# Three edits at the first tile of a retention and maxout kernel: where the tables are issued, when the scores are made, how the last products are ordered

## The chip, the cores and the metric

The kernel runs on one core of a Trainium2 chip. The metric is the device time of one execution in microseconds (us). A core has a matrix engine (TensorE, PE in the profile; its weight loads are PEld), a vector engine (VectorE, DVE), a scalar engine (ScalarE, ACT), a general engine (GpSimd, POOL) and a queue engine (SyncE, SP). Each works through its own instructions in order[...]. Products land in PSUM, eight banks of 128 x 512 fp32.

## The reference

```python
scores = scale * (q @ k.T)                      # 8 batches, 8 heads, 576 positions, 64 wide
ret = scores * gamma[h] ** (i - j), for i >= j  # 0 otherwise
attn = ret @ v
x = attn.transpose(0, 2, 1, 3).reshape(4608, 512)
h = maximum(maximum(x @ w1, x @ w2), x @ w3)    # w1, w2, w3: 512 x 768
out = h @ w_out                                 # w_out: 768 x 512
```

The four weight matrices come in as float64 (read as pairs of 32-bit words) and are made into float32 on the chip. All products are in fp32.

## The kernel before, in words

The 4608 positions are cut into 36 chunks of 128 (`C`), and four chunks make a tile of 512 (`NT`): nine tiles. The attention is done in its recurrent form, chunk by chunk:

- `load(g)` (L160) issues the transfers of k, q and v of a chunk from SP's queue. From chunk 7 on (`BY_PE`), q and k also come in blocks of 32 (`load_blocks`, L147).
- `decay_values(g)` (L164, POOL) scales v by the table `gk`, and gives `vd`.
- `transposes(g)` makes k and q transposed: below chunk 7 on PE (`kt`, `qt`, L181) with copies by ACT (L183); later by DVE (L175).
- `scores(g)` forms `s` on PE in two banks (L191), and DVE multiplies them with the causal mask into `st` (L194).
- `values(chunks, new_states)` adds `st` by `vd` (L244), forms `kv` for the next state (L211), adds the part of the old state (L256), and DVE scales the result by the table `gq` into `xT` (L263), the transposed x of the tile. `keep` (L219, L221, POOL L222) makes the next state with the table `gs`.

`convert(n)` takes n steps of a generator which turns the float64 pieces of the weights (128 x 512 each) into float32: 18 pieces of w1 to w3 and six of w_out, each four steps, with DVE (L431, L436, L442, L447, L453) and ACT (L432, L434, L437). Each finished piece frees a buffer for the next piece's load (`load_weights`, L311 and L305, SP).

Tile 0 takes the weights as they come: `up_plain` (L553) makes one 128 x 512 block of one of the three products, and DVE takes the maximum (L556; for w1 a copy by ACT, L557). A pair of blocks is a unit, and there are nine units. Then `down` makes the four row blocks of the output, each one bank with six products over all of the hidden units (L544), a copy by ACT and a store. From tile 1 on each unit is done by Strassen's scheme with seven half-sized products (`up`, L495, tiles x, y and z), and `downs` likewise (L367). These need sums of weight blocks (`weight_sums(n)` for a unit, L474 and L475 on DVE, L476 and L477 on POOL), sums of x (L273 to L276), sums of w_out (`sums_of_outs`) and of the hidden units (`sums_of_hidden`). `chores` is a list of such small works, and `up` takes one of them at three places (`chore()`).

The order of instructions is written by hand. A prelude at the end of the kernel's function (L601 to L631) does the first four chunks. The main loop (L670) then does, for each of twelve steps of a tile, the attention work that `steps(t + 1)` puts there for the next tile, and one stretch of the tile's own work (`ffn(t)` up to its next `yield`).

PSUM is divided into `ps_r` (four banks), `ps_x` and `ps_y` (two each).

Of the kernel before, what the change touches and what calls it, by code (L numbers as in the profile page):

```python
# [34 lines left out]
FP32 = mybir.dt.float32  # L35
# [7 lines left out]
C = 128  # L43
NT = 4 * C
# [7 lines left out]
def kernel(  # L52
# [14 lines left out]
    nc = tc.nc  # L67
    P = 128
    B, H, S, D = q.shape
    N, DM = out.shape  # L70
    DF = moe_w1.shape[1]
    NP = H // 2
    NG = B * S // C
    NDC = DM // P
    NF = DF // P
    CPT = NT // C
# [11 lines left out]
    opool = ctx.enter_context(tc.tile_pool(name="opool", bufs=2))  # L88
    while_converting = ExitStack()
    wraw = while_converting.enter_context(tc.tile_pool(name="wraw", bufs=WAHEAD))  # L90
    wtmp = while_converting.enter_context(tc.tile_pool(name="wtmp", bufs=4))
    ps_r = ctx.enter_context(tc.tile_pool(name="ps_r", bufs=4, space=PSUM))
    ps_x = ctx.enter_context(tc.tile_pool(name="ps_x", bufs=2, space=PSUM))
    ps_y = ctx.enter_context(tc.tile_pool(name="ps_y", bufs=2, space=PSUM))
# [3 lines left out]
    gq = const.tile([P, NP, C], FP32, name="gq")  # L98
    gs = const.tile([P, NP, D], FP32, name="gs")
# [21 lines left out]
    for r in sorted({start_of(g) for g in range(NG)} - {0, None}):  # L121
        m = masks[r] = const.tile([C, C], FP32, name=f"causal{r}")
# [15 lines left out]
    def load_blocks(g, *blocks):  # L138
        for n, src in (("q", q), ("kx", k)):

            if 0 in blocks:
                raws[n, g] = raw.tile([P, NP, C // 32, 32], FP32, tag=n, name=n + "raw", bufs=3 if n == "q" else 2)
            t = raws[n, g]
            for blk in blocks:
                b, pos = divmod(g * C + 32 * blk, S)
                for a in range(4):
                    nc.sync.dma_start(  # L147
                        t[32 * a:32 * a + 32, :, blk, :],
                        src[b, a // 2::2, pos:pos + 32, 32 * (a % 2):32 * (a % 2) + 32].rearrange("p j i -> j p i"))

    def load(g, *between):
        if g >= BY_PE and ("q", g) not in raws:
            load_blocks(g, *range(C // 32))
        for n, src in (("k", k), ("q", q), ("v", v)) if g < BY_PE else (("k", k), ("v", v)):
            if n == "v":
                for t, what in between:
                    nc.sync.dma_start(t, what)
            t = raws[n, g] = raw.tile([C, H, D], FP32, tag=n, name=n + "raw", bufs=4 if n == "k" else 3)
            for row, b, pos, m in spans(g):
                nc.sync.dma_start(t[row:row + m], src[b, :, pos:pos + m, :].rearrange("h p d -> p h d"))  # L160

    def decay_values(g):
        t = vds[g] = vpool.tile([C, H, D], FP32, tag="vd", name="vd")
        nc.gpsimd.tensor_tensor(t[:], raws.pop(("v", g))[:], gk[:].unsqueeze(2).to_broadcast([C, H, D]),  # L164
                                op=ALU.mult)
# [4 lines left out]
    def transposes(g):  # L170
        both = qks[g] = {}
        if g >= BY_PE:
            for n in ("k", "q"):
                t = both[n] = att.tile([P, NP, C], FP32, tag=n + "T", name=n + "T", bufs=2 if n == "k" else 3)
                nc.vector.transpose(t[:].rearrange("a p c -> a (p c)"),  # L175
                                    raws.pop(("kx" if n == "k" else n, g))[:].rearrange("a p b i -> a (p b i)"))
            return
        for n, src in (("k", raws["k", g]), ("q", raws.pop(("q", g)))):
            pt = ps_r.tile([P, NP, C], FP32, tag="r", name=n + "t")
            for p in range(NP):  # L180
                nc.tensor.transpose(pt[:, p, :], pair(src, p), ident[:C, :C])  # L181
            t = both[n] = att.tile([P, NP, C], FP32, tag=n + "T", name=n + "T", bufs=2 if n == "k" else 3)
            nc.scalar.copy(t[:], pt[:])  # L183

    def scores(g):
        qT, kT = qks[g]["q"], qks[g]["k"]
        s = [ps_r.tile([C, NP, C], FP32, tag="r", name=f"s{j}") for j in range(2)]
        for p in range(NP):
            for j in range(2):
                r = slice(D * j, D * (j + 1))  # L190
                nc.tensor.matmul(s[j][:, p, :], lhsT=kT[r, p, :], rhs=qT[r, p, :], start=True, stop=True)  # L191
        st = sts[g] = att.tile([C, 2, NP, C], FP32, tag="st", name="st", bufs=2)
        for j in range(2):
            nc.vector.tensor_tensor(st[:, j], s[j][:], masks[start_of(g)][:].unsqueeze(1).to_broadcast([C, NP, C]),  # L194
                                    op=ALU.mult)
# [4 lines left out]
    def half(j):  # L200
        return slice(D * j, D * (j + 1))
# [91 lines left out]
    units = [(fp, i) for fp in range(NF // 2) for i in range(3)]  # L293
    pieces = [(i, 2 * fp + e) for fp, i in units for e in range(2)] + [("out", fb) for fb in range(NF)]
    w_sb, wT, bits, to_load = {}, {}, {}, deque(pieces)
# [17 lines left out]
    late, chores = {}, deque()  # L313
# [152 lines left out]
    def weight_sums(n):  # L466
        if n >= len(units):
            return
        fp, i = units[n]
        half = [slice(0, DM // 2), slice(DM // 2, DM)]  # L470
        b11, b21 = (w_sb[i, 2 * fp][:, r] for r in half)
        b12, b22 = (w_sb[i, 2 * fp + 1][:, r] for r in half)
        t1, t2, t4 = (late["pool"].tile([P, DM // 2], FP32, name=f"T{m}_{i}_{fp}")[:] for m in (1, 2, 4))
        nc.vector.tensor_tensor(t1, b12, b11, op=ALU.subtract)  # L474
        nc.vector.tensor_tensor(t2, b22, t1, op=ALU.subtract)  # L475
        nc.gpsimd.tensor_tensor(b12, b22, b12, op=ALU.subtract)  # L476
        nc.gpsimd.tensor_tensor(t4, b21, t2, op=ALU.subtract)  # L477
        wT[fp, i] = {1: b11, 2: b21, 3: b22, 4: t4, 5: t1, 6: t2, 7: b12}
# [3 lines left out]
    def convert(n):  # L482
        for _ in range(n):
            next(converting, None)
# [53 lines left out]
            nc.vector.tensor_tensor(h[:, f0, :], h[:, f0, :], tmp[:, 0:2, :].rearrange("p a b -> p (a b)"), op=ALU.max)  # L538
        yield

    def down(t, h, m):
        ps = ps_y.tile([P, DM], FP32, tag="y", name="down")
        for fb in range(NF):
            nc.tensor.matmul(ps[:], lhsT=h[:, fb, m * P:(m + 1) * P], rhs=w_sb["out", fb],  # L544
                             start=(fb == 0), stop=(fb == NF - 1))
        osb = opool.tile([P, DM], FP32, tag="osb", name="osb")
        nc.scalar.copy(osb[:], ps[:])
        nc.sync.dma_start(out[t * NT + m * P:t * NT + (m + 1) * P, :], osb[:])

    def up_plain(t, h, fb, i):  # L550
        ps = (ps_x, ps_y)[fb % 2].tile([P, NT], FP32, tag="xy"[fb % 2], name="up")
# [7 lines left out]
    def ffn(t):  # L559

        h = hpool.tile([P, NF, NT], FP32, tag="h", name="h")
        for n, (fp, i) in enumerate(units):
            if t == 0:
                for fb in (2 * fp, 2 * fp + 1):
                    maximum = up_plain(t, h, fb, i)
                    convert(4 if i > 0 else 8 if fb % 2 == 0 else 6 if fp == 0 else 4)
                    maximum()
            else:
                if t == 1 and n == 0:
                    sums_of_outs()  # L570
                for _ in up(t, h, fp, i):
                    pass
                if i == 2:
                    sums_of_hidden(h, fp)
            yield
        if t == 0:
            convert(4 * len(pieces))
            while_converting.close()
            late["pool"] = ctx.enter_context(tc.tile_pool(name="late", bufs=1))
            for m in range(NT // P):  # L580
                down(t, h, m)
                for n in [[0, 1, 2], [3, 4, 5], [6], [7, 8]][m]:
                    weight_sums(n)
                if m < NT // P - 2:
                    yield
        else:
            chore(len(chores))
            for n, _ in enumerate(downs(t, h)):
                if n in (1, 3):
                    yield  # L590
        yield


    def tables():
        for j in range(2):
            yield gs[half(j)], state_decay[half(j), :, half(j)]
        for c in range(2):
            for b in range(2):
                yield gq[half(c), b::2, :], out_decay[half(b ^ c), NP // 2 * c:NP // 2 * (c + 1), :]

    warm(6)  # L601
    load(0)
    load(1)
    load(2, *tables())
    load(3)
    load_weights(2)
    load(4)
    load_weights(4)
    decay_values(0)
    transposes(0)  # L610
    warm(2)
    decay_values(1)
    scores(0)
    transposes(1)
    values([0], [0])
    decay_values(2)
    scores(1)
    transposes(2)
    values([1], [1])
    decay_values(3)  # L620
    scores(2)
    transposes(3)
    convert(2)
    values([2], [2])
    convert(2)
    scores(3)
    decay_values(4)
    convert(2)
    values([3], [3])
    transposes(4)  # L630
    convert(4)  # L631

    def steps(t):
# [93 lines left out]
```

## Time and profile before

| | |
|---|---|
| time, median of 3 runs | 804.61 us (803.94 to 806.73) |
| span of the profiled run | 802.5 us |
| PE, DVE, ACT, POOL busy | 98%, 52%, 22%, 18% |
| mean granted clock of PE | 0.995 |
| DMA over the span | 73 GB/s, from 0 to 40 us some 200 |
| first up product of tile 0 | at 34.73 us |
| first down product of tile 0 | at 107.51 us |
| first product of tile 1 | at 134.30 us |

The profile is one execution. Busy time is the time in which an engine had an instruction under way. Matmuls overlap, so that a busy PE need not be at its peak; whether it is, is seen from the number of products in a stretch and the time of one. An idle time is put down to what ended it ("<-" and the instruction that released it).

### The profile page before, as it was taken

What the parts mean: (1) busy time and instruction counts of PE and PEld (TensorE: products, weight loads), DVE (VectorE), ACT (ScalarE), POOL (GpSimd) and SP (SyncE); (2) the same over time, 40 slices, a digit from 0 to 9 for tenths busy, and PEclk for the clock granted to TensorE, in tenths of its full rate; (3) what the DMA queues carried; (4) which work ended last, traced back from release to release, by engine and by line L of the source; (5) the groups of instructions that cost most, each with busy time, mean ns of one, the idle gap of its engine ahead of it and who ended that gap; (6) DMA issues with size and microseconds to landing.
All of it is one profiled execution on the core that took longest, in us unless ns stands there. A gap on an engine that the chain in (4) does not pass through costs nothing.

```text
span 802.5 us, 13705 instructions
## 1 busy us (share of the span) xinstructions
PE 789.0 (98%) x5128; PEld 646.7 (81%) x5128; DVE 418.8 (52%) x833; ACT 173.7 (22%) x401; POOL 141.8 (18%) x158
## 2 busy tenths in 40 slices
PE   7899989999999999999999999999999999999998
PEld 6555436888888888888888888888888888888887
DVE  1799998545353635353544444553546344633341
ACT  2476631111111101111111111111111021111211
POOL 2200229201301121111211121112101201110000
PEclk9999999999999999999999999999999999999999
DMA  8986633333233322343233333333323323001001
GB/s 189 227 206 162 183 81 97 56 57 57 75 66 56 59 60 63 58 78 67 57 54 57 58 91 57 57 56 89 58 53 58 74 57 71 1 14 40 1 1 52
DMA packets 237506, 59.27 MB, mean 74 GB/s; under 512 B 218240, under 2 KB 236160, under 8 KB 237440
## 3 DMA queue, kind: packets, MB, share of 16 engines
q1 hardware_dynamic: 237296, 58.40, 33.3%
q8 instruction: 40, 0.66, 0.4%
q14 instruction: 26, 0.21, 0.1%
q10 hardware_dynamic: 144, 0.00, 0.0%
HBM read 48.89 MB, written 9.44 MB: 73 GB/s over the span
## 4 chain that ended last, share of the span: by engine, by line
PE 86%; DVE 5%; DMA 4%; SPq 3%; issue 1%; ACT 0%; DVEq 0%
PE x L495 32%; PE z L495 16%; PE dx L367 11%; PE y L495 8%; PE dz L367 5%; PE o L244 4%; PE s L191 3%; PE dy L367 3%; PE down L544 2%; SPq L160 2%; PE o L256 2%; PE kv L211 2%; DMA bits<-in_moe_w_dram 1%; DVE expo L447 1%; SPq L311 1%
## 5 line engine op out<-in xcount | busy, mean ns | idle before, releaser
L495 PE MATMUL x<-S,T 128*128 128x256 f32 x576 | 147.9, 379 | 0.0
L495 PEld LDWEIGHTS x<-S,T 128*128 128x128 f32 x576 | 109.1, 190 | 15.3 <-ACT p L500 0.2
L345 POOL TENSOR_TENSOR H<-h 128x256 f32<-128x256 f32 x24 | 21.3, 886 | 331.8 <-DVE h L538 331.8
L495 PE MATMUL x<-xT,w 128*128 128x256 f32 x288 | 76.1, 387 | 0.0
L495 PE MATMUL x<-S,w 128*128 128x256 f32 x288 | 74.3, 380 | 0.0
L525 DVE TENSOR_TENSOR tmp<-x,p 128x256 f32<-128x256 f32 x48 | 20.4, 425 | 103.1 <-PE x L495 103.1
L495 PE MATMUL z<-xT,T 128*128 128x256 f32 x288 | 74.0, 379 | 0.0
L495 PE MATMUL y<-xT,w 128*128 128x256 f32 x288 | 73.9, 379 | 0.0
L495 PE MATMUL z<-S,w 128*128 128x256 f32 x288 | 73.9, 379 | 0.0
L263 DVE TENSOR_TENSOR xT<-o,gq 128x512 f32<-128x512 f32 (+1 forms) x40 | 23.7, 633 | 86.5 <-PE o L256 81.1
L500 ACT COPY p<-x 128x256 f32<-128x256 f32 x72 | 26.8, 373 | 192.0 <-PE x L495 192.0
L553 PE MATMUL up<-xT,w 128*128 128x512 f32 x144 | 63.4, 595 | 0.0
L495 PEld LDWEIGHTS z<-xT,T 128*128 128x128 f32 x288 | 54.4, 189 | 8.0 <-ACT p L500 0.3
L495 PEld LDWEIGHTS y<-xT,w 128*128 128x128 f32 x288 | 54.7, 190 | 7.4
L495 PEld LDWEIGHTS z<-S,w 128*128 128x128 f32 x288 | 54.7, 190 | 7.4
L495 PEld LDWEIGHTS x<-xT,w 128*128 128x128 f32 x288 | 53.0, 190 | 9.6 <-issue 1.5
L495 PEld LDWEIGHTS x<-S,w 128*128 128x128 f32 x288 | 49.4, 189 | 13.2 <-issue 1.5
L222 POOL TENSOR_TENSOR state<-state,gs 128x256 f32<-128x256 f32 x24 | 22.0, 916 | 183.4 <-DVE state L221 179.5
L553 PEld LDWEIGHTS up<-xT,w 128*128 128x128 f32 x144 | 26.8, 190 | 31.6 <-issue 29.3
L194 DVE TENSOR_TENSOR st<-s,causal 128x512 f32<-128x512 f32 x72 | 45.0, 684 | 8.0 <-PE s L191 7.1
L500 ACT COPY u<-x 128x256 f32<-128x256 f32 x72 | 26.8, 373 | 99.8 <-PE x L495 88.8
L164 POOL TENSOR_TENSOR vd<-vraw,gk 128x512 f32<-128x512 f32 x36 | 38.3, 1064 | 45.8 <-DMA vraw<-in_v_dram 45.8
(92 smaller groups left out, 1099.4 us busy)
## 6 DMA issues: line engine op xcount, KB each, us to landing
out_dram<-osb SPq DMA_DIRECT2D x35, 256.0 KB, 2.1
kraw<-in_k_dram SPq DMA_DIRECT2D x32, 256.0 KB, 3.0
vraw<-in_v_dram SPq DMA_DIRECT2D x32, 256.0 KB, 3.5
qraw<-in_q_dram SPq DMA_DIRECT2D x464, 16.0 KB, 1.9
kxraw<-in_k_dram SPq DMA_DIRECT2D x464, 16.0 KB, 1.8
bits<-in_moe_w_dram SPq DMA_DIRECT2D x18, 256.0 KB, 4.4
bits<-in_moe_w_dram SPq DMA_DIRECT2D x36, 128.0 KB, 4.2
bits<-in_moe_w_out_dram SPq DMA_DIRECT2D x6, 512.0 KB, 4.8
```

Source lines behind the costliest of these rows:

```text
L164: nc.gpsimd.tensor_tensor(t[:], raws.pop(("v", g))[:], gk[:].unsqueeze(2).to_broadcast([C, H, D]), op=ALU.mult)
L191: nc.tensor.matmul(s[j][:, p, :], lhsT=kT[r, p, :], rhs=qT[r, p, :], start=True, stop=True)
L194: nc.vector.tensor_tensor(st[:, j], s[j][:], masks[start_of(g)][:].unsqueeze(1).to_broadcast([C, NP, C]), op=ALU.mult)
L222: nc.gpsimd.tensor_tensor(t[:], t[:], gs[:], op=ALU.mult)
L244: nc.tensor.matmul(o[n % 2][half(c), m, n // 2, :], lhsT=vds[g][:, h, :], rhs=sts[g][:, h % 2, h // 2, :], start=m == 0 and n < 2, stop=be ...
L263: nc.vector.tensor_tensor(xT[t][:, b::2, i * C:(i + len(chunks)) * C].rearrange("p u (m c) -> p u m c", c=C), o[b][:].rearrange("p m u c - ...
L345: chores.append(lambda: (pool(s3, a11, a21, op=ALU.subtract), pool(s4, a12, s2, op=ALU.subtract)))
L367: nc.tensor.matmul(out[m], lhsT=hS[n](fp)[:, m * P:(m + 1) * P], rhs=late["T"][n][:, fp, :], start=first and fp == 0 and (m == 0 or last a ...
L495: nc.tensor.matmul(out[:], lhsT=w[:, d * P:(d + 1) * P], rhs=xS[t][n][:, d, :], start=first and d == 0, stop=d == 1, skip_group_check=True)
L500: nc.scalar.copy(c[:], src[:])
L525: nc.vector.tensor_tensor(c22, x[:], p7[:], op=ALU.add)
L553: nc.tensor.matmul(ps[:], lhsT=w_sb[i, fb][:, dc * P:(dc + 1) * P], rhs=xT[t][:, dc, :], start=(dc == 0), stop=(dc == NDC - 1))
```

## The change: what it does

It has three parts.

1. *Tables by ScalarE's queue.* The tables `gs` and `gq` (six transfers of 64 KB) were issued by SP between q and v of chunk 2. They are now issued by ACT, before its first copy. SP loads chunks 0 to 4 and the weights with nothing in between.
2. *The first chunks' scores a chunk ahead.* In the prelude, the scores of a chunk come before the values of the chunk before it, so that DVE can mask them while PE is at the other. For this the transposes of chunks 0 to 4 take the banks of `ps_x`, and the scores have `ps_r` for themselves. transposes(4) now stands before values(3), and the first conversion steps come after the scores of chunk 3.
3. *Last products of tile 0 by blocks of units in four banks.* `downs_plain` has all four row blocks open at once, and goes over the six hidden blocks outermost. A w_out piece is needed only when its block is come to. Conversion steps are spread evenly (four for each up product), and the last two pieces of w_out are converted during the first two blocks. The sums of weights of units 0 to 2 are made in the last three blocks, those of units 3 to 8 in tile 1 (the second tile) as chores.

```diff
-    def load(g, *between):
+    def load(g):
...
-            if n == "v":
-                for t, what in between:
-                    nc.sync.dma_start(t, what)
...
-            pt = ps_r.tile([P, NP, C], FP32, tag="r", name=n + "t")
+            pool, tag = (ps_r, "r") if g > CPT else (ps_x, "x")
+            pt = pool.tile([P, NP, C], FP32, tag=tag, name=n + "t")
...
-    def down(t, h, m):
-        ps = ps_y.tile([P, DM], FP32, tag="y", name="down")
+    def downs_plain(t, h):
+        ps = [(ps_x, ps_y)[m % 2].tile([P, DM], FP32, tag="xy"[m % 2], name="down") for m in range(NT // P)]
         for fb in range(NF):
-            nc.tensor.matmul(ps[:], lhsT=h[:, fb, m * P:(m + 1) * P], rhs=w_sb["out", fb],
-                             start=(fb == 0), stop=(fb == NF - 1))
-        osb = opool.tile([P, DM], FP32, tag="osb", name="osb")
-        nc.scalar.copy(osb[:], ps[:])
-        nc.sync.dma_start(out[t * NT + m * P:t * NT + (m + 1) * P, :], osb[:])
+            for m, b in enumerate(ps):
+                nc.tensor.matmul(b[:], lhsT=h[:, fb, m * P:(m + 1) * P], rhs=w_sb["out", fb],
+                                 start=(fb == 0), stop=(fb == NF - 1))
+                if fb == NF - 1:
+                    osb = opool.tile([P, DM], FP32, tag="osb", name="osb")
+                    nc.scalar.copy(osb[:], b[:])
+                    nc.sync.dma_start(out[t * NT + m * P:t * NT + (m + 1) * P, :], osb[:])
+            yield
...
-                    convert(4 if i > 0 else 8 if fb % 2 == 0 else 6 if fp == 0 else 4)
+                    convert(4)
...
-            convert(4 * len(pieces))
-            while_converting.close()
-            late["pool"] = ctx.enter_context(tc.tile_pool(name="late", bufs=1))
-            for m in range(NT // P):
-                down(t, h, m)
-                for n in [[0, 1, 2], [3, 4, 5], [6], [7, 8]][m]:
-                    weight_sums(n)
-                if m < NT // P - 2:
-                    yield
+            convert(6)
+            for fb, _ in enumerate(downs_plain(t, h)):
+                convert(4 if fb < 2 else 4 * len(pieces))
+                if fb in (1, 3):
+                    yield
+                if fb == 3:
+                    while_converting.close()
+                    late["pool"] = ctx.enter_context(tc.tile_pool(name="late", bufs=1))
+                if fb > 2:
+                    weight_sums(fb - 3)
+            for n in range(3, len(units), 2):
+                chores.extend([partial(weight_sums, n), partial(weight_sums, n + 1), lambda: None])
...
-    def tables():
-        for j in range(2):
-            yield gs[half(j)], state_decay[half(j), :, half(j)]
-        for c in range(2):
-            for b in range(2):
-                yield gq[half(c), b::2, :], out_decay[half(b ^ c), NP // 2 * c:NP // 2 * (c + 1), :]
-
+    for j in range(2):
+        nc.scalar.dma_start(gs[half(j)], state_decay[half(j), :, half(j)])
+    for c in range(2):
+        for b in range(2):
+            nc.scalar.dma_start(gq[half(c), b::2, :], out_decay[half(b ^ c), NP // 2 * c:NP // 2 * (c + 1), :])
     warm(6)
-    load(0)
-    load(1)
-    load(2, *tables())
-    load(3)
+    for g in range(CPT):
+        load(g)
     load_weights(2)
-    load(4)
+    load(CPT)
     load_weights(4)
     decay_values(0)
     transposes(0)
     warm(2)
     decay_values(1)
     scores(0)
     transposes(1)
+    scores(1)
+    decay_values(2)
     values([0], [0])
-    decay_values(2)
-    scores(1)
     transposes(2)
+    scores(2)
     values([1], [1])
     decay_values(3)
-    scores(2)
     transposes(3)
+    scores(3)
     convert(2)
     values([2], [2])
     convert(2)
-    scores(3)
+    transposes(4)
     decay_values(4)
     convert(2)
     values([3], [3])
-    transposes(4)
     convert(4)
```

## The prediction

> **What bounds the kernel now.** I read the page's busy rows first, then a table of windows by stage, then TensorE's timeline from 10 to 36 us and from 106 to 136 us, then the list of waits of TensorE.
>
> ```profile
> 0.00:34.73 34.73, 26.31 (x297) 22.75 (x297) 14.36 (x30) 10.15 (x16) 8.89 (x17) 0.90 0.84 200
> 34.73:107.50 72.77, 72.77 (x338) 36.46 (x337) 71.49 (x129) 47.50 (x73) 7.89 (x6) 1.00 0.71 180
> 107.50:134.30 26.80, 24.74 (x130) 12.03 (x128) 26.39 (x37) 5.21 (x8) 19.65 (x21) 1.00 0.41 94
> 134.30:802.50 668.20, 665.21 (x4369) 575.46 (x4367) 306.55 (x640) 110.87 (x305) 105.38 (x115) 1.00 0.27 55
> ```
>
> The columns are busy us of PE, PEld, DVE, ACT and POOL, then granted clock, DMA share and GB/s. From 34.73 us (first up product of tile 0) to 107.50 PE is never idle. The 144 records at L553 are 72 products, two records each; at 0.4325 us a record (16 take 6.92 to 6.97) they are 62.3 us, and the attention pieces between them 10.2 us: 72.5 of 72.77. So PE is at its work there and not only shown busy; but DVE has 71.49 busy, nearly as full. After 134.30 PE runs to the end but for the last 3 us. What can be gained lies before 34.73 and between 107.5 and 134.3.
>
> ```profile
> 12.51 0.60 PE L181 MATMUL qt<-ident,qraw 128*128 128x128 f32 x4
> 16.75 2.26 PE L244 MATMUL o<-st,vd 128*64 128x128 f32 x15 [3.65 <-DVE st L194]
> ...
> 20.65 1.16 PE L191 MATMUL s<-qT,kT 64*128 64x128 f32 x16
> ...
> 22.77 1.40 PE L244 MATMUL o<-st,vd 128*64 128x128 f32 x15
> ...
> 25.27 1.16 PE L191 MATMUL s<-qT,kT 64*128 64x128 f32 x16
> 29.66 2.08 PE L244 MATMUL o<-st,vd 128*64 128x128 f32 x15 [3.23 <-DVE st L194]
> ...
> 33.80 0.66 PE L181 MATMUL kt<-ident,kraw 128*128 128x128 f32 x4
> ```
>
> Two stalls, 3.65 and 3.23 us, both on the masked scores `st`. The same group (o, kv, o) takes 25.27 - 22.77 = 2.50 us undisturbed, but 3.90 after the first stall and 4.14 after the second: another 1.40 and 1.64. In one-us windows the granted clock is 0.50 from 17 to 20 us and from 31 to 33.
>
> ```profile
> DVE xT L263 <- DMA gq<-in_out_decay_dram: 5.4, 2, 5.3
> PE down L544 <- DVE h L556: 1.4, 1, 1.4
> PE down L544 <- DVE w_out L453: 0.7, 1, 0.7
> ```
>
> The first stall is DVE's queue: xT of chunk 0 waits for the table gq until 14.67 and 15.25, and chunk 1's `st` stands behind it (15.93). The second: DVE converts the first weight piece from 23.05 to 28.8 ahead of chunk 3's `st`. The last two lines are the stall at the first down block, which needs all six converted w_out pieces at once.
>
> **What the Trainium skill says.** "DMA: Bandwidth & Descriptors", Issuing engines are not separate DMA queues: a second issuing engine saves only the sequencer's issue time; transfers share the same 16 engines. The trace agrees that issue time matters here: tables hold SP's queue from 8.41 to 13.4 us, and DMA share falls to 0.30 to 0.56 between 11 and 15 us. "TensorE: Matmul & The Clock Gate", Part 1: after an idle window of about 3.4 us the clock is halved. The trace agrees (0.50 after 3.65 and 3.23, still 1.00 after 1.40). "SBUF — State Buffer", Who interferes with whom: DVE with two SBUF inputs and a reading GpSimd operation block each other. The trace agrees: L474 takes 0.42 us alone, 0.94 beside POOL.
>
> **The change part by part.** Times below are the profile's; totals are estimates from them.
>
> 1. *Start of the ups.* Gone, if tables and scores come in time: 3.65 + 3.23 + 1.40 + 1.64 = 9.9 us. Four things come back.
>  (a) ACT now issues six table transfers before its table load and its first copy. One issue of such a size took 0.60 to 0.97 us at SP, once 1.35. ACT issued gk at 0.81 in 0.42; six at 0.65 end at 5.2, the load of 1.28 at 6.5, and kT of chunk 0 is copied at 6.5 in place of 5.26. Bounds: 1.2 us (0.6 each) to 5.4 (1.35 each, ACT free at 10.7). Behind the issues stand the copies kT, qT; PE's s waits for these. I take 1.2: small transfers took 0.60 at the median.
>  (b) 384 KB of tables now run beside chunk 0 and 1. At the 235 to 268 GB/s seen there these are 1.5 us, but v of chunk 2 (landed about 16.9) comes at about 13.7, since the hole of 11 to 15 us closes; chunk 3 at about 17, weight piece 0 at about 19, piece 1 at about 21. PE needs chunk 2's at about 13 to 21, so nothing is added.
>  (c) The transposes of the first five chunks go to the two ps_x banks, which kv also uses. qt of chunks 2, 3 and 4 waits for DVE to read the kv before: xT twice (0.7) and state (0.4) after the last o, less kt (0.55) on PE: about 0.5 each, 1.5 in all; bounds 0.5 and 2.5.
>  (d) transposes(4) stood after values(3), so kt and qt (0.93) hid xT of chunk 3 (0.76). Now it stands before, and the first up waits bare: 0.9.
>  DVE converts pieces 0 and 1 in the gaps, with xT of chunks 2 and 3 behind them; they land some 3 us before DVE comes to them, so no wait is added. Sum: 9.9 - 1.2 - 1.5 - 0.9 = 6.3 us; the ups start at 28.4.
>
> 2. *Ups.* PE's 72.8 us stay. The extra conversions that ran ahead (8 and 6 steps) become 4 for each product. Steps are a quarter of a piece, a piece costs DVE 2.6 us (0.34 + 0.34 + 0.6 + 0.7 + 0.6). Piece n is then written before the maximum of product n-2, that is one product (3.5 us) before PE needs it. DVE's load from start to the last maximum: 19 pieces 49.4, 12 maxima 7.2, st 4.8, states, xT and transposes 3.4, blocking by GpSimd about 4.5 (as before): 69.3 of 72.8. PE stays the bound; DVE's lead is shorter, not gone. Transfers: q and k blocks of chunk 7 must be in by about 82; SP issued the last at 88 before (needed at 97.8), and comes about 12 us earlier, as loads wait for fewer conversions. Hidden.
>
> 3. *Last products of tile 0.* 24 products at 0.865 = 20.8 us plus values 3.39 make 24.2; 26.8 were used: 2.6 us lost. With the unit of w_out outermost, the last two pieces are needed 16 products = 13.8 us into the stage, and DVE has them about 8 us in: the stall goes, -2.6. What comes: all four banks end together. ACT's third copy waits for the store of the first (two osb buffers; 2.1 us to landing), the fourth for the second, and behind them stands the copy p1 of tile 1, for which x of product 6 waits. The first block ends 2.6 us before the last, copy 0.6, issue and landing 2.5: p1 is read about 0.5 us late. +0.5 (0 to 1.5).
>
> 4. *Weight sums.* Units 0 to 2 run after values, 6 to 8 as chores in tile two. DVE takes 2 x 0.42 (0.95 contested), POOL 1.75 a unit; two such units in one up unit of 6.05 us give DVE at most 3.8 and POOL 3.5. DVE was 73% busy at 130 to 150, its other work there about 3.5 of 6 a unit, so it just fits. Product 6 of unit 0 needs t2, 8.6 us after values end; DVE has it after xT, S1, S2 at about 4.8; w of product 7 comes from POOL at 6.8, needed at 9.5. I charge 0.4 for late sums behind c22 (0 to 3).
>
> Sum: -6.3 - 2.6 + 0.5 + 0.4 = -8.0: 804.6 - 8.0 = 796.6 us.
>
> **The rivals.** *R1: DVE becomes the bound.* For: 71.49 of 72.77 busy. If its blocking costs twice the 4.5 us, its 73.8 exceeds PE's 72.8, and the short lead leaves waits at single products; with 3 more for a late chunk 7 some 4 us of the gain are lost: 800.6. Against: before, its lead grew from 0.8 us at piece 1 to 12 us at piece 17, while 3.5 extra pieces (9 us) were done.
> *R2: ACT's queue is the new wait.* Issues of 1.35 us move every copy by 5.4 in place of 1.2: 800.8. For: SP's issues of whole chunks rose to 1.62 in that stretch. Against: small ones stayed mostly at 0.60.
> *R3: slower.* Tile two starved: each of the units 0 to 2 late by 4 us through sums on DVE and POOL that must come in order, 12 us in all: 808.6. For: POOL is 100% busy from 116 to 135. Against: To chores of the same kind ran in tile two (1.5 pairs in a unit) with no PE wait.
>
> **How the numbers follow.** The forecast (795 to 798.5) 0.62; R1 0.17; R2 0.12; R3 0.04; better than forecast (put-backs at their low ends: up to 3 us less) 0.05. The range 793.6 to 801.5: below, the low ends of (c), 3 and 4 and a hidden (d); above, R1 and R2 with a little more. Faster by over 0.3% (below 802.2): 0.92, which leaves 0.04 for the upper tails of R1 and R2, within 0.3%; slower: 0.04, R3.
>
> **What would show it.** Right: no PE wait over 1.5 us before the first up, clock at 1.00 between 10 and 35 us, first up at 28 to 29.5; 72 to 73.5 us from there to the first down; no wait on w_out; 24 to 25 us from the first down to tile 1's first x. Wrong: kT of chunk 0 copied after 8 us (R2); PE waiting for L451's w within the ups (R1); waits of x, y or z for T or p1 in the first three units of tile 1 (R3).

## The result, and the profile after

The changed kernel takes 800.66 us (median of six runs, 799.61 to 800.93); the kernel before, on the same chip, 803.67 (six runs; the 804.61 given above is the median of the first three of them). The ratio is 0.9954, with a 95% interval of 0.9938 to 0.9971: about 3 us or 0.5% faster, where 8 us were forecast. A second measurement of the same kernel (below) gave 0.9959 (0.9945 to 0.9972).

The same table of windows as before, with its borders at the first up product, the first down product and the first product of tile 1. The columns are busy us of PE, PEld, DVE, ACT and POOL, granted clock, DMA share and GB/s.

```profile
0.00:30.59 30.59, 22.75 (x297) 19.06 (x297) 13.41 (x29) 10.46 (x17) 8.61 (x17) 1.00 0.91 217
30.59:103.44 72.85, 72.85 (x336) 36.52 (x337) 67.14 (x122) 43.64 (x66) 6.40 (x6) 1.00 0.73 177
103.44:127.64 24.20, 24.20 (x130) 12.20 (x129) 18.43 (x29) 8.74 (x13) 6.15 (x6) 1.00 0.46 104
127.64:797.90 670.26, 665.86 (x4369) 575.13 (x4367) 315.43 (x656) 111.36 (x306) 118.35 (x130) 1.00 0.27 56
```

Beside the table of before, border by border (us):

| stage | before | after | difference | forecast |
|---|---|---|---|---|
| to the first up product | 34.73 | 30.59 | -4.14 | -6.3 |
| ups of tile 0 | 72.77 | 72.85 | +0.08 | 0 |
| last products of tile 0 | 26.80 | 24.20 | -2.60 | -2.6 |
| tile 1 to the end | 668.20 | 670.26 | +2.06 | +0.9 |
| span | 802.5 | 797.9 | -4.6 | -8.0 |

The two profiled executions differ by 4.6 us and the medians by 3.0, because the profile of before is of a run of 804.17 us (0.5 above its median) and that of after is of the fastest of its six (1.05 below its median).

PE's timeline of the changed kernel before the first up shows what came in place of the two stalls on `st` (start, us, what, and in brackets the idle time before and what ended it):

```profile
7.73 1.16 PE L189 MATMUL s<-qT,kT 64*128 64x128 f32 x16 [0.64 <-ACT qT L181]
...
11.26 1.16 PE L189 MATMUL s<-qT,kT 64*128 64x128 f32 x16 [0.67 <-ACT qT L181]
...
14.78 0.66 PE L179 MATMUL qt<-ident,qraw 128*128 128x128 f32 x4 [0.29 <-DVE state L217]
16.12 1.16 PE L189 MATMUL s<-qT,kT 64*128 64x128 f32 x16 [0.68 <-ACT qT L181]
...
20.59 0.63 PE L179 MATMUL qt<-ident,qraw 128*128 128x128 f32 x4 [0.64 <-PE kt L179]
21.89 1.16 PE L189 MATMUL s<-qT,kT 64*128 64x128 f32 x16 [0.67 <-ACT qT L181]
...
26.36 0.63 PE L179 MATMUL qt<-ident,qraw 128*128 128x128 f32 x4 [0.64 <-PE kt L179]
...
30.59 7.10 PE L555 MATMUL up<-xT,w 128*128 128x512 f32 x16 [1.52 <-ACT expo L432]
```

No single wait is long, and the clock stays at 1.00. But there are four waits of the scores for the copy qT that was just made (the first of them, of chunk 0, comes from ACT's table issues), three of qt for a bank of `ps_x`, and one before the first up. Two of the three waits of qt are put down to PE's own kt; DVE reads the bank as `state`, which ends at 20.48 and 26.25, and qt starts 0.11 us after each. The wait before the first up is put down to ACT, but DVE's queue shows what it fits: xT of chunk 3.

```profile
28.02 1.42 DVE L451 TENSOR_TENSOR w<-mant,expo 128x512 f32<-128x512 f32 x1
...
30.03 0.74 DVE L261 TENSOR_TENSOR xT<-o,gq 128x256 f32<-128x256 f32 x2
```

The product that xT needs (o) ends near 29.1. xT stands behind the conversion of piece 0, whose last two instructions were slow (1.22 and 1.42 us, where 0.69 is usual), and behind the first two instructions of piece 1 (29.36 to 30.03).

In tile 1 there are two waits in the first unit, from 127.64 to 135.51. Both are for the bank `x`: ACT copies it after the unit's first product (`p1`), and DVE adds it into the hidden units after product 5 (`c22`). Products 6 and 3 write to `x` again and wait for these two.

```profile
127.64 1.03 PE L493 MATMUL x<-xT,w 128*128 128x256 f32 x4
128.50 1.03 PE L493 MATMUL y<-xT,w 128*128 128x256 f32 x4
130.08 1.13 PE L493 MATMUL x<-S,T 128*128 128x256 f32 x4 [0.55 <-ACT p L498]
...
134.54 1.13 PE L493 MATMUL x<-S,w 128*128 128x256 f32 x4 [0.74 <-DVE h L523]
135.51 1.03 PE L493 MATMUL x<-xT,w 128*128 128x256 f32 x4
```

The unit takes 7.87 us; before, the same unit took 6.10, with no wait:

```profile
134.30 1.03 PE L495 MATMUL x<-xT,w 128*128 128x256 f32 x4
...
140.40 1.03 PE L495 MATMUL x<-xT,w 128*128 128x256 f32 x4
```

The two printed waits are 1.29 us of the difference; the rest is lost in the spacing of the products around them (product 6 starts 1.58 us after the product before it, where the kernel before has 0.87). So 1.77 of the 2.60 us that the last products gave are paid back at once.

### The profile page after: what moved, and what is told of

Same layout as the page of the kernel before. It is cut to its first block, busy times and chain, and to the rows that moved or that the text cites. A ratio compares the mean times of both kernels' runs of the same rounds, so it can differ in the third digit from the quotient of the medians.

```text
span 797.9 us, 13707 instructions
## 1 busy us (share of the span) xinstructions
PE 785.7 (98%) x5128; PEld 642.9 (81%) x5128; DVE 414.4 (52%) x833; ACT 174.2 (22%) x401; POOL 139.5 (17%) x158
## 5 line engine op out<-in xcount | busy, mean ns | idle before, releaser
L220 POOL TENSOR_TENSOR state<-state,gs 128x256 f32<-128x256 f32 x24 | 20.1, 836 | 187.5 <-DVE state L219 187.5
```

Source lines behind the costliest of these rows:

```text
L220: nc.gpsimd.tensor_tensor(t[:], t[:], gs[:], op=ALU.mult)
```

## The experiments

Each kernel was timed against the kernel before in interleaved runs on the same chip; ratios are to the kernel before. There were three groups, each with its own runs of the kernel before (medians 803.58 to 803.70); a difference to the changed kernel is one of medians from different groups, with the repeat of the changed kernel (800.43) as its time, and is not called shown where both the intervals of the ratios and the runs themselves overlap. The theory after the result, called A in the expectations: part 1 brings the gain, and parts 2 and 3 mostly turn one wait into another.

### The three parts one by one

*Part 1 alone* (tables by ACT, all else as before):

```diff
-    load(2, *tables())
+    load(2)
...
+        nc.scalar.dma_start(gs[half(j)], state_decay[half(j), :, half(j)])
...
+            nc.scalar.dma_start(gq[half(c), b::2, :], out_decay[half(b ^ c), NP // 2 * c:NP // 2 * (c + 1), :])
```

> Part 1 alone: the six table transfers by ACT, all else as before. Theory A (the table issue at SP caused the first stall; part 2 pays back most of what it removes): PE's first stall of 3.65 us and its slow stretch go, the second stall on st of chunk 3 stays at 3 to 4 us, first up at 29 to 31 us, some 4 us faster than before, as much as the whole change gains in the prelude. Theory B (the second stall is half of the gain, so part 2 is needed): first up at 32.5 us or later, 2 us faster at the most.

Measured: 800.22 us, ratio 0.9957 (0.9944 to 0.9971): as fast as the whole change. The first up comes at 32.24, between the two expectations. The first stall is gone and the second is there in full; a new wait of s of chunk 0 stands behind ACT's table issues:

```profile
7.69 1.85 PE L191 MATMUL s<-qT,kT 64*128 64x128 f32 x16 [1.32 <-ACT qT L183]
...
26.48 2.26 PE L244 MATMUL o<-st,vd 128*64 128x128 f32 x15 [3.24 <-DVE st L194]
...
32.24 2.31 PE L553 MATMUL up<-xT,w 128*128 128x512 f32 x5
```

After the second stall the group o, kv, o takes 4.32 us (26.48 to 30.80). After the new wait the granted clock is 0.50 from 8 to 11 us too, and from s of chunk 0 to the first o it takes 3.68 us, before 2.31. The mean clock of this profiled run is 0.994, that of the five others 0.998, so this profile holds more of the slow clock than the other runs. The rest of its gain is later: the wait on w_out in the last products is gone, that on `h` is as before, so these take 25.92 in place of 26.80.

*Part 2 alone* (scores a chunk ahead and transposes in `ps_x`, the tables still issued by SP; the prelude's diff is that of the change):

> Part 2 alone: scores a chunk ahead with transposes in ps_x, tables still issued by SP. Theory A: xT of chunk 0 still waits for gq until about 15 us, and the second qt of ps_x behind it; waits of s on the copy qT (0.67 us each) and of qt on ps_x come in; first up at 32 to 34 us, 1 to 2.5 us faster than before. Theory B: the second stall of 3.23 us and its slow clock go and nothing comes back: first up at 30 us, 4.5 us faster.

Measured: 804.18 us, ratio 1.0002 (0.9992 to 1.0011): nothing, where Theory A expected 1 to 2.5 us and Theory B 4.5. PE's first up comes at 34.44, and these waits came in:

```profile
PE qt L182 <- DVE state L220: 3.4, 1, 3.4
PE s L192 <- ACT qT L184: 2.2, 4, 0.7
PE up L554 <- ACT expo L435: 1.5, 1, 1.5
PE qt L182 <- PE kt L182: 1.3, 2, 0.6
```

(us in total, times, longest.) DVE still waits for gq, now with the state of chunk 0 behind it; and since kv and the transposes share `ps_x`, the table's lateness reaches PE by the bank. After the wait of 3.36 us the clock is 0.50 from 16 to 22 us; qt, s and o take 1.12, 2.08 and 1.97 us there, and 0.63, 1.16 and 1.09 a chunk later.

*Part 3 alone* (the diff of `downs_plain`, `convert` and `weight_sums`):

> Part 3 alone: even conversion steps, last products in four banks, weight sums of units 3 to 8 in tile two. Theory A: first up at 34.7 as before, ups 72.8 us, the last products 24.2 in place of 26.8 us, tile 1 1.5 to 2 us longer by the waits on p1 and c22: net 0.6 to 1.1 us faster. Theory B (even steps leave DVE without a lead): waits of up products on L453 in the ups, and slower than before by 1 us or more.

Measured: 803.67 us, ratio 1.0003 (0.9995 to 1.0011): nothing, where Theory A expected 0.6 to 1.1 us, though the last products take 24.2 us (107.68 to 131.87) and tile 1's first unit is 1.76 us longer, as it said. The next tile's first product comes at 218.61, before at 218.92: from 2.4 us ahead it falls back to 0.3 ahead. The ups take 72.8 us with no wait on w, so the even conversion steps cost nothing.

*Parts 1 and 2* (the changed kernel with the last products, the conversion steps and the weight sums as before):

> Parts 1 and 2 without part 3. Theory A (part 2 adds the 1.6 us between the first ups of part 1 alone, 32.24, and the whole change, 30.6, and part 3 adds 0.8 us or less): first up at 30.6 to 31 us, and the last products still 26 to 27 us long with a wait on w_out or h; 1 us faster to 0.5 us slower than the whole change. Theory B (part 3's 2.6 us count in full): 2 us or more slower than the whole change.

Measured: 799.56 us, ratio 0.9948 (0.9934 to 0.9963); first up at 30.73, last products 26.33 us with 1.40 and 0.20 us of waits on h and w_out, tile 1's first unit 6.09 us. It is no slower than the whole change, whose ratio on the same terms is:

> The whole change once more, on the same chip as its parts: about 3 to 4.6 us faster than before; the first up at 30.6 us. If the parts add up, the sum of the three single gains is this gain; Theory A says it is less than the sum, since parts 1 and 2 remove the same time.

Measured: 800.43 us, ratio 0.9959 (0.9945 to 0.9972), first up at 30.94. The parts' medians against 803.61 are -3.4, +0.6 and +0.1, in sum -2.7, and the whole -3.2: it is not less than the sum, as Theory A had it, and the two don't differ by more than the noise. By the borders of the trace part 2 adds 1.5 us to part 1 at the first up and 1.0 at tile 2's first product (215.56 and 214.54). But the slow clock from 8 to 11 us costs the profile of part 1 alone 1.4 us, and the ratios (0.9957 and 0.9948) have intervals that overlap, as have the runs; so a gain of part 2 on top of part 1 is not shown. Part 3 adds 0.2 to 0.5 at tile 2 (214.54, and 214.38 and 214.03 in the two profiles of the whole).

### What part 2 pays back

*Transposes ahead of the values before:*

```diff
     scores(1)
     decay_values(2)
+    transposes(2)
     values([0], [0])
-    transposes(2)
     scores(2)
+    transposes(3)
     values([1], [1])
     decay_values(3)
-    transposes(3)
     scores(3)
     convert(2)
     values([2], [2])
     convert(2)
-    transposes(4)
     decay_values(4)
-    convert(2)
     values([3], [3])
-    convert(4)
+    transposes(4)
+    convert(6)
```

> The changed kernel with the transposes of chunks 2 and 3 before the values of chunks 0 and 1, those of chunk 4 after the values of chunk 3, and the conversion of piece 1 after these. Theory A (what the prelude pays back are s waiting for the copy qT, 0.67 us three times, qt waiting for its ps_x bank, 1.6 us, and the bare wait of 1.5 us before the first up): all three go, waits on transfers of k and q of chunks 2 and 3 of about 1 us in all come in, first up at 27.5 to 29 us in place of 30.6 to 30.9, some 2 to 3 us faster than the changed kernel. Theory B (the prelude is bound by the transfers or by DVE's conversion of the first pieces): first up at 30 us or later, no gain.

Measured: 797.66 us, ratio 0.9925 (0.9911 to 0.9939): 2.8 us faster than the changed kernel. First up at 27.71. In PE's timeline the scores of chunks 2 and 3 start without a wait, and what remains stands on DVE's first conversions:

```profile
15.22 1.16 PE L189 MATMUL s<-qT,kT 64*128 64x128 f32 x16
...
19.42 1.16 PE L189 MATMUL s<-qT,kT 64*128 64x128 f32 x16
...
23.52 1.11 PE L242 MATMUL o<-st,vd 128*64 128x128 f32 x16 [0.86 <-DVE xT L261]
...
27.71 3.60 PE L555 MATMUL up<-xT,w 128*128 128x512 f32 x8
32.02 3.70 PE L555 MATMUL up<-xT,w 128*128 128x512 f32 x8 [0.71 <-DVE w L451]
```

So the short waits of part 2 were worth about 3 us at the first up. The ups are 0.9 us longer (27.71 to 101.47), so that 2.0 to 2.3 us are left at the first down product. The order of the instructions was the cause, not the transfers; but the edit moves the transposes and two conversion steps together, and what each is worth is not shown.

*gq issued by ACT after its first two copies* (this one is about the cost of part 1's issues):

```diff
+    transposes(0)
+    for c in range(2):
+        for b in range(2):
+            nc.scalar.dma_start(gq[half(c), b::2, :], out_decay[half(b ^ c), NP // 2 * c:NP // 2 * (c + 1), :])
```

(and taken out before `warm(6)`.)

> The changed kernel with the four transfers of gq issued by ACT after its first two copies (gs before, as it is). Theory A (while ACT issues, SP's own issues are held: v of chunk 0 is issued at 3.5 us, before at 1.93): v of chunk 0 and k of chunk 1 are issued a microsecond or more earlier, kT of chunk 0 is copied at 5.3 in place of 6.6, and SP is held later, between 7 and 10 us; first up 0 to 1 us earlier. Theory B (SP's start is late for another cause): v of chunk 0 at 3.5 us as in the changed kernel.

Measured: 800.21 us, ratio 0.9961 (0.9948 to 0.9974), the first up at 30.49, so no gain over the changed kernel; but SP's start changed as Theory A said. SP's issues in the changed kernel, and with gq late (start, us):

```profile
1.30 0.58 SPq L157 DMA_DIRECT2D qraw<-in_q_dram  x1
3.62 0.37 SPq L157 DMA_DIRECT2D vraw<-in_v_dram  x1
5.02 0.37 SPq L157 DMA_DIRECT2D kraw<-in_k_dram  x1
```

```profile
1.30 0.58 SPq L157 DMA_DIRECT2D qraw<-in_q_dram  x1
1.93 0.77 SPq L157 DMA_DIRECT2D vraw<-in_v_dram  x1
2.74 1.03 SPq L157 DMA_DIRECT2D kraw<-in_k_dram  x1
```

While ACT issues its six transfers (1.29 to 5.28), SP's queue stands still between its own, from 1.88 to 3.62 and from 3.99 to 5.02. The later hold that Theory A expected didn't come: while ACT issues gq from 6.43 to 9.98, SP's issues follow each other with no gap over 0.05 us, at 0.85 to 1.62 us each. What was won at the start is lost at ACT: the copies of chunk 1 stand behind the late issues, and s of chunk 1 waits 1.90 us for qT.

### What part 3 pays back

*The first three units' sums before xT*, in DVE's gap:

```diff
-                if fb in (1, 3):
-                    yield
-                if fb == 3:
+                if fb == 2:
                     while_converting.close()
                     late["pool"] = ctx.enter_context(tc.tile_pool(name="late", bufs=1))
-                if fb > 2:
-                    weight_sums(fb - 3)
+                for n in [[], [], [0], [1, 2], [], []][fb]:
+                    weight_sums(n)
+                if fb in (1, 3):
+                    yield
```

> The changed kernel with the weight sums of units 0 to 2 made in the third and fourth block of the last products, ahead of xT, where DVE is idle for 5.6 us. Theory A (DVE's late c22 is why product 3 of tile 1's first unit waits 0.7 to 0.9 us; DVE runs sums, transposes and chores without a gap from 120.8 to 137): that wait goes, the wait on p1 of 0.6 us stays; 0.7 to 1 us faster than the changed kernel. Theory B (the chores in tile two are the cause, wherever the first three units' sums stand): the wait stays.

Measured: 798.52 us, ratio 0.9937 (0.9923 to 0.9951), 1.9 us faster than the changed kernel, where 0.7 to 1 was expected; its slowest run (799.12) is below the fastest of the changed kernel (799.32). The wait on c22 is gone and the first unit of tile 1 takes 6.57 us, which is 1.3 us of it; where the rest comes from is not shown. The wait on p1 is 0.21, but that wait varies by itself: it is 0.55 and 0.36 in the two profiles of the changed kernel, and 0.21 with gq late. DVE now has time to spare there: it waits 2.50 us for p1, where in the changed kernel it ran without a gap.

*Four output buffers:*

```diff
-    opool = ctx.enter_context(tc.tile_pool(name="opool", bufs=2))
+    opool = ctx.enter_context(tc.tile_pool(name="opool", bufs=4))
```

> The changed kernel with four output buffers in place of two. Theory A: ACT's copies of the third and fourth row block wait for no store, p1 of tile 1 is copied in time, the wait of product 6 of 0.4 to 0.6 us goes; 0.5 us faster than the changed kernel or less, since DVE's c22 may be as late as before. Theory B (p1 waits for ACT's copies themselves, not for the stores): the wait stays at 0.4 or more.

Measured: 799.32 us, ratio 0.9948 (0.9934 to 0.9963). The wait on p1 is gone, and the unit is as long as before, 7.86 us:

```profile
127.61 1.03 PE L493 MATMUL x<-xT,w 128*128 128x256 f32 x4
134.50 1.13 PE L493 MATMUL x<-S,w 128*128 128x256 f32 x4 [1.55 <-DVE h L523]
135.47 1.03 PE L493 MATMUL x<-xT,w 128*128 128x256 f32 x4
```

The whole wait is now c22's. So DVE sets the end of this unit, and the late p1 was in its shadow. It is the same the other way round with the transposes ahead: there p1 is 1.56 us late, c22 is no longer waited for, and the unit takes 7.87 us again. By the medians the kernel is still 1.1 us faster, but intervals and runs overlap, so this is not shown, and it would not be in this unit. In the repeat of the changed kernel, ACT waits for a store near 723 us too, and with it p1, by which PE lost another 0.33 us; with four buffers no wait for p1 remains after tile 1. That may account for a part of it; the first profile of the changed kernel has no such wait either.

```profile
723.71 0.65 ACT L415 COPY osb<-dx 128x256 f32<-128x256 f32 x2 [11.29 <-DMA out_dram<-osb]
724.24 0.39 ACT L498 COPY p<-x 128x256 f32<-128x256 f32 x1
```

*All sums in the last blocks, no chores:*

```diff
-                    weight_sums(fb - 3)
-            for n in range(3, len(units), 2):
-                chores.extend([partial(weight_sums, n), partial(weight_sums, n + 1), lambda: None])
+                    for n in range(3 * (fb - 3), 3 * (fb - 2)):
+                        weight_sums(n)
```

> The changed kernel with all nine units' weight sums in the last three blocks, three in each, behind xT and the sums of x on DVE, and none as chores. Theory A (it is the order of the sums on DVE after the values that makes tile 1's first unit wait): 9 times some 1.7 us stand ahead of DVE's first additions of tile 1, which come near 140 us in place of 132.3; PE waits 6 to 9 us in tile 1's first unit; 4 to 8 us slower than the changed kernel. Theory B (the chores between the products are what holds PE): the waits of 0.7 to 0.9 us on c22 go, faster than the changed kernel.

Measured: 810.66 us, ratio 1.0085 (1.0071 to 1.0100). It is 10.2 us slower than the changed kernel, and PE waits 10.03 us for c22 in tile 1's first unit; 4 to 8 and 6 to 9 were expected. After this wait the clock is 0.50 too (140 to 147 us). The eighteen instructions on DVE run from 123.92 to 140.65 in one row at some 1.73 us for a unit, since POOL's half runs beside them. It is the order on DVE after the values that counts; made as chores, the sums of units 3 to 8 cost much less.

### Together

*Transposes ahead, sums before xT and four output buffers in one kernel* (the run best):

> The changed kernel with the transposes ahead, the first three sums before xT, and four output buffers. Theory A (three separate waits on PE's path): first up at 27.7, tile 1's first unit 6.1 to 6.3 us, the gains of 2.8, 1.9 and up to 1.1 us add up but for some tenths; 795 to 796 us, 7.5 to 8.5 us faster than before. Theory B (DVE's conversion now sets the pace in the ups): new waits on w in the ups of 2 us or more, 797 or more.

Measured: 795.35 us, ratio 0.9900 (0.9883 to 0.9917): 8.3 us faster than the kernel before and 5.1 faster than the changed kernel. First up at 27.43, the last products 24.2 us, tile 1's first unit 6.10 us with no wait. The ups take 73.77 us, with one wait on w of 0.71: Theory B's mechanism is there, at less than half of the 2 us it named.

*The same with gq late:*

> As the run best, with the four transfers of gq issued by ACT after its first two copies. Theory A (the transfers of chunks 2 and 3 are now what PE waits for, and SP issues them earlier when it isn't held at the start): first up 0.3 to 1 us earlier than in best. Theory B (xT of chunk 2 and the conversion of piece 0 on DVE set the first up): within 0.3 us of best.

Measured: 797.14 us, ratio 0.9914 (0.9898 to 0.9930): 1.8 us slower than without, which neither expectation had. s of chunk 1 waits 2.29 us for qT, and after that PE's clock falls (windows of 4 us; the clock is the third number from the right). At the values of chunk 1, PE is 1.8 us behind the run without (18.86 and 17.07), and still at tile 2's first product (211.82 and 210.02).

```profile
8.00:12.00 4.00, 1.62 (x16) 1.17 (x18) 1.29 (x2) 1.07 (x2) 1.04 (x1) 1.00 1.15 270
12.00:16.00 4.00, 4.00 (x36) 3.55 (x34) 1.29 (x2) 1.17 (x2) 1.04 (x1) 0.58 1.13 275
```

## Why the forecast of the time came out too low

The time of 800.66 us lies in the range, but 4.1 us above the forecast of 796.6; the gain was 3.0 and not 8.0. (The forecast started from 804.6; the median of six runs of the kernel before is 0.9 lower.) That the range held was in part luck: its upper end was there for R1 and R2, whose times, 800.6 and 800.8, nearly hit the measured one, and neither happened. kT of chunk 0 was copied at 6.60, and no up product waited for w. Other terms took their place. Of the signs of being right, the clock, the ups, w_out and the last products came true; the first up (28 to 29.5 said) did not, and the wait of 1.52 us before it is just over the 1.5 that was allowed.

- *What bounds the kernel.* Right. PE has 72.85 of 72.85 us in the ups, and the changes of time lie before the ups, in the last products and in tile 1's first unit, but for 0.3 us after tile 2's first product.
- *Step 1, the start: the step that failed.* The gross part was right: both stalls and both slow stretches went. (a) was nearly right (copy of kT at 6.60, 6.5 said; s of chunk 0 starts 0.9 us later, 1.2 said), and (c) was right (0.29 + 0.64 + 0.64 = 1.57; 1.5 said). But the sum had no term for the scores that now stand right behind their own transposes: qt, copy, s is a chain of two engines, and s waits 0.67 us each for chunks 1, 2 and 3, 2.0 in all. Before, o, kv and o stood between. And (d) was 1.52 in place of 0.9. The prediction had the conversions of pieces 0 and 1 ahead of xT on DVE and added no wait, since the pieces land in time; but piece 0, slowed on DVE, and the first steps of piece 1 hold xT of chunk 3 back. These four make 0.9 + 1.57 + 2.0 + 1.5 = 6.0 where 3.6 were put back, and 9.9 - 4.1 = 5.8 were measured. The agreement is not exact bookkeeping: (b), put at nothing, adds the 0.28 us for which qt of chunk 1 waits for its load, and the groups o, kv, o became some 0.4 us shorter each (2.09 in place of 2.50), which nobody had counted. With the transposes ahead and the conversion of piece 1 later, the first up moved by 2.9 to 3.2 us; that shows these terms together, and not each by itself.
- *Step 2, the ups.* Right: no wait on w with the even steps. R1 fell.
- *Step 3, the last products.* Right to the tenth (-2.60), and the mechanism of the wait on p1 too: ACT's third copy waits 1.82 us for the store of the first. Its size (0.55; 0.5 said) is a near hit by luck, since the second profile of the changed kernel has 0.36. And it isn't a term of its own: with four output buffers it is gone and the unit is still 7.86 us long.
- *Step 4, the sums: the second term that was too small.* 0.4 was charged for late sums behind c22. The unit is 1.77 us longer, p1 included, 0.9 said for both. What was overlooked is that DVE is idle for 5.56 us before xT and then takes xT, S, three units' sums, two transposes and two more units' sums in one row, each unit's pair some 1.75 us beside POOL. In the kernel before, DVE filled this time with the sums of six units, and the values ended 10.4 us before tile 1's first product (123.89 and 134.30); in the changed kernel they end 7.0 us before it (120.67 and 127.64). The run with the first three units' sums before xT shows that the idle time was the place for them. The mechanism of R3 was thus there, at a seventh of its size, and so was its sign, a wait for p1.
- *From trace to median.* The trace had -4.6 against -8.0. The other 1.6 us to the median of -3.0 are the scatter of the two profiled runs. It was 0.9 us between two profiles of the changed kernel (797.9 and 798.8): 0.35 of it was there by the first up, the rest after tile 1's first unit, where the second profile has 0.3 us more of waits on p1.

The forecast credited all three parts. The runs show that part 1 brings the gain; parts 2 and 3, each by itself or on top of the others, add nothing that the medians can tell. The forecast time of 796.6 was reached only when the orders behind steps 1 and 4 were changed, together with the output buffers (795.35).

## What to carry to other kernels

When an order is changed to hide one latency, write down for each instruction what it now stands directly behind: a product that moves next to the copy it reads pays that chain every time (here 0.67 us, three times). A stage that becomes shorter on the bounding engine only counts if the next stage's inputs on the other engines keep up; here the idle time of the vector engine ahead of its longest row was the place to put work. And a wait that one run shows can lie in the shadow of another; take both away before counting either.

## What the runs showed of the hardware that was not expected

- Issuing from a second queue held the first at the start: with six issues on ACT between 1.29 and 5.28 us, SP's third issue began at 3.3 to 3.6 us in all runs with that order, at 1.93 or 1.94 without. Four issues on ACT from 6.43 to 9.98 us (gq late) left no gap in SP's. What the two queues share there the traces don't show.
- The half clock did not go by the length of the last idle time alone. It came after 3.65 and 3.23 us in the kernel before, after 3.36 with part 2 alone, and after 2.29 in the last experiment (0.50 from 13 to 16 us), but not after 1.90 at the same place with gq late. And with part 1 alone it came after 1.32 us (0.50 from 8 to 11 us), less than the 1.40 that the prediction found harmless and well under the idle window of about 3.4 us that it went by.
